# Sparse attention and a gated MLP on one core: the scores of three batches in three parts, and a new order on four engines

## The chip, the core and the metric

The kernel runs on one core of a Trainium2 chip. Five engines of that core work side by side, each through its own queue of instructions in order: TensorE (matmuls, PE in the profile), VectorE (DVE), ScalarE (ACT), GpSimd (POOL) and SyncE (SP, which only issues transfers here). GpSimd issues the loads, SyncE the stores and one kind of transfer inside the chip. The metric is the device time of one execution in microseconds; lower is better.

## The reference

```python
# q, k, v: (4 batches, 8 heads, 768 positions, 64), float32
k_sum = k.reshape(B, H, 24, 32, D).max(axis=3)
v_sum = v.reshape(B, H, 24, 32, D).mean(axis=3)
scores_l = scale * q @ k^T, kept where |i - j| < 16
scores_s = scale * q @ k_sum^T + log(32)
a = softmax(concat([scores_l masked, scores_s]))
attn = a @ concat([v, v_sum])
x = attn as (3072 tokens, 512)
h = x @ w_in                                  # 512 to 2048
g = h * clip(h + 3, 0, 6) / 6
out = g @ w_out                               # 2048 to 512, float32
```

Every position attends to its neighbours within 16 and to 24 block summaries; the result goes through one gated MLP over all 3,072 tokens.

## The kernel before

Queries are taken in 12 blocks of 64 per head. A block sees a window of 96 keys and the 24 maxima of the blocks of keys, so its scores are 120 rows: `kaug` holds 96 window keys and 24 maxima for each block, `qT` the queries with their positions shifted by 16, `at` the exponentials of the scores, `vaug` the values with a column of ones and the 24 block sums.

The work is cut into steps, and a key names each instruction (or short group) of a step: `s111.0` is instruction 0 of step s111. The steps are

- `c`: constants; `K`, `Q`, `V`, `H`, `I`, `O`: loads by GpSimd (k, q, v, the shifted part of v, w_in, w_out);
- `k0` to `k3`, `q0` to `q7`: transposes of k and q on TensorE and copies from PSUM (batch 0, and q of batch 1); `w10` to `w33`: transposes, copies and maxima of k (and of q for batches 2 and 3) on VectorE and ScalarE;
- `s`: scores on TensorE, exp on ScalarE, the mask on VectorE. Batch 0: `s0` pair of heads, half; in its first half the mask is added by two matmuls called cover (instruction 0), and the scores are instruction 1. Batches 1 to 3: `scores4`, keys `s` batch, pair of pairs, half. One call takes 6 blocks of 4 heads, 48 matmuls of 32 rows and 64 columns, into both `S` slots, then two exps of 768 elements a row and two masks;
- `h`: copies of the halo of v inside `vaug`; `u`: block sums of v and their spreading; `v`: values, reciprocal, scale, then transposes of the result (`xtr`) and copies into x. `v41` is the second half of batch 0. From x number 4 on (`LATE`), the transposes are done by VectorE (`blocks`, into y) and 16 transfers of SyncE per x (`move`, instructions 4 to 7 of `v201`, `v211`, `v301`, `v311`);
- `F` s `x` ft: x number s (0 to 7, 384 tokens each) times one 128-column slice of w_in, four matmuls of 384 columns, relu on ScalarE (instruction 1), gate on VectorE (instruction 2). For s = 0 and ft below 5 (`SPLIT`) the four matmuls are separate keys;
- `G` s ts `x` 0: 128 tokens times w_out in four parts of four matmuls, a copy (instruction 4) and a store (instruction 5).

PSUM holds three `h` slots, one `o` and two `S` slots of two banks. A slot is given to a step when its first instruction is issued and comes free after its last.

The text `ORDER` lists all keys, and the kernel issues its instructions in exactly that sequence, so each engine's queue is the part of the list that belongs to it. `:A` and `:D` choose ScalarE or VectorE where either can do a copy. Tokens that start with `~`, `-`, `_` or `=` are fillers (`keep`): matmuls of the constant tile idle into a free slot, whose result nobody reads. `~n`, `-n` and `_n` are n matmuls of 512, 128 and 64 columns; `=n` is one of n times 64 columns.

Of the kernel before, what the change touches and what calls it, by code (L numbers as in the profile page):

```python
# [37 lines left out]
F0x8.1 F0x8.2 F0x5.1 I0.0 F0x5.2 F0x11.0 F0x1.0 F0x11.1 F0x11.2 F0x1.1 F0x1.2 F0x1.3 F0x1.4 F0x1.5 v410.0 v410.1 F0x7.0 F0x7.1
F0x7.2 v410.2 F0x10.0 F0x10.1 I12.0 F0x13.0 F0x13.1 F0x15.0 F0x15.1 F0x13.2 F0x10.2 v411.3 v411.4:D v410.3 v410.4:A F0x15.2
F0x14.0 F0x14.1 F0x14.2 F0x9.0 F0x9.1 F0x9.2 F0x0.0 F0x0.1 F0x2.0 F0x2.1 K13.0 K10.0 c.12:A F0x0.2 K12.0 K11.0 w10.0 Q1w1.0  # L40
F1x14.0 F1x14.1 F1x14.2 F1x4.0 F1x4.1 F1x4.2 F1x2.0 F1x2.1 F1x2.2 w10.1:D F0x2.2 F0x2.3 F0x2.4 F0x12.0 F0x12.1 F0x12.2 F1x8.0
# [772 lines left out]
```

## Time and profile before

| what | value |
| --- | --- |
| median of 3 runs | 217.21 us (217.05 to 217.39) |
| profiled execution, span | 215.4 us |
| TensorE busy | 207.6 us, 96% |
| VectorE busy | 162.1 us, 75% |
| ScalarE busy | 136.0 us, 63% |
| GpSimd busy | 49.7 us, 23% |
| data moved by transfers | 22.68 MB |

The time of the profiled execution is known as its span only, from the first to the last instruction; the runs' times also hold what lies around it. In rows of the timeline the first number is the start in us from the span's start, the second the length, then the engine, the line, the operation and its tiles; in square brackets stands the idle time before it and what ended it. In grouped rows the two numbers behind the bar are the busy time in us and the mean duration in ns.

### The profile page before, as it was taken

Reading aid. Unit: us, or ns where it says so; the run is one execution under the profiler, and the core shown is the slowest. Engines: PE = TensorE matmul, PEld = TensorE weight load, DVE = VectorE, ACT = ScalarE, POOL = GpSimd, SP = SyncE. Lnnn points to the kernel's source line nnn. Section 1 sums busy time; section 2 is a strip of 40 time slices with the busy share of each in tenths; the row PEclk is TensorE's granted clock in tenths of the full one; section 3 lists DMA queues with packets and bytes.
Section 4 is the critical chain, followed back from the end, with each engine's and each line's share of the span. In section 5 each row is a group of like instructions: output and inputs, shape, how many; then the busy total and the mean of one; then the engine's idle time right before and its main releaser. Section 6 shows DMA issues by size and latency. Waiting matters only on the chain.

```text
span 215.4 us, 6065 instructions
## 1 busy us (share of the span) xinstructions
PE 207.6 (96%) x2521; PEld 119.9 (56%) x2548; DVE 162.1 (75%) x318; ACT 136.0 (63%) x264; POOL 49.7 (23%) x66
## 2 busy tenths in 40 slices
PE   7999999999999999999999999999999999999993
PEld 7556656655555565565555555555555555564442
DVE  6889889999899999898899889887865555640021
ACT  3879778887898988756578696566345355520110
POOL 7968347905753244000000000000000000000000
PEclk9999999999999999999999999999999999999999
DMA  5999999999999999930334234113314300013123
GB/s 75 161 155 188 204 187 171 191 201 163 204 160 194 181 121 151 107 146 11 37 37 143 27 37 110 49 22 38 70 21 80 76 0 17 34 49 122 52 85 134
DMA packets 91724, 22.68 MB, mean 105 GB/s; under 512 B 82224, under 2 KB 88752, under 8 KB 91696
## 3 DMA queue, kind: packets, MB, share of 16 engines
q0 software_dynamic: 62288, 14.41, 71.9%
q1 hardware_dynamic: 29264, 7.80, 15.3%
q8 instruction: 20, 0.33, 0.6%
q10 hardware_dynamic: 144, 0.07, 0.1%
q14 instruction: 8, 0.07, 0.1%
HBM read 28.82 MB, written 6.29 MB: 163 GB/s over the span
## 4 chain that ended last, share of the span: by engine, by line
PE 82%; SPq 5%; DMA 4%; issue 2%; DVE 2%; POOL 2%; ACT 1%; ACTq 0%; POOLq 0%
PE h L666 36%; PE o L683 29%; PE h L683 5%; SPq L648 4%; DMA first<-in_q_dram 3%; PE S L623 3%; PE S L512 2%; DMA out_dram<-ot 1%; ACT vaug L241 1%; POOL first L305 1%; PE S L636 1%; PE S L666 1%; PE h L581 1%; PE S L489 1%; PE S L553 1%
## 5 line engine op out<-in xcount | busy, mean ns | idle before, releaser
L666 PE MATMUL h<-x,win 128*128 128x384 bf16 x500 | 91.1, 326 | 0.1
L670 ACT ACTIVATE r<-h 128x384 f32<-128x384 f32 x125 | 58.7, 492 | 38.8 <-PE h L666 36.8
L671 DVE SCALAR_TENSOR_TENSOR g<-r,h 128x384 bf16<-128x384 f32 x125 | 65.9, 546 | 22.6 <-ACT r L670 20.0
L683 PE MATMUL o<-wout,g 128*128 128x512 bf16 x309 | 78.0, 379 | 1.9 <-issue 0.8
L666 PEld LDWEIGHTS <-win 128*128 128x128 bf16 x512 | 48.7, 98 | 35.5
L683 PEld LDWEIGHTS <-g 128*128 128x128 bf16 x400 | 38.4, 98 | 37.6 <-issue 0.3
L520 ACT ACTIVATE at<-S 120x768 bf16<-120x768 f32 x24 | 18.6, 810 | 5.5 <-PE S L512 5.4
L241 ACT COPY ot<-o 128x512 f32<-128x512 f32 x17 | 10.0, 587 | 15.4 <-PE o L683 14.2
L521 DVE TENSOR_TENSOR at<-at,mask 96x768 bf16<-96x768 bf16 x24 | 12.6, 549 | 2.0 <-ACT at L520 1.6
L605 DVE TENSOR_TENSOR xn<-S,rc 128x768 bf16<-128x768 f32 x14 | 13.3, 950 | 0.3
L343 POOL DMA_DIRECT2D vaug<-in_v_dram x10 | 11.9, 1194 | 0.4 <-DMA first<-in_k_dram 0.2
L241 DVE COPY ot<-h 128x512 f32<-128x512 f32 x2 | 1.3, 686 | 13.7 <-PE h L683 13.7
L683 PE MATMUL h<-wout,g 128*128 128x256 bf16 (+1 forms) x64 | 11.4, 326 | 0.0
L467 DVE TENSOR_REDUCE red<-kaug 128x24 bf16<-128x768 bf16 x12 | 11.2, 943 | 0.1
L241 ACT COPY vaug<-vaug 32x640 bf16<-32x640 bf16 (+3 forms) x17 | 8.9, 574 | 0.6 <-DMA vaug<-in_v_dram 0.3
L241 ACT COPY vaug<-vs 24x1536 bf16<-24x1536 bf16 x6 | 8.8, 1468 | 0.6 <-DVE vs L241 0.5
L782 PE MATMUL o<-idle 128*128 128x64 bf16 (+2 forms) x70 | 7.5, 287 | 1.1 <-DVE idle L287 1.1
L455 DVE STREAM_TRANSPOSE kaug<-kraw 128x768 bf16<-128x768 bf16 x8 | 8.1, 1025 | 0.3 <-PE S L512 0.3
L623 PEld LDWEIGHTS <-at 120*64 120x64 bf16 x336 | 6.3, 111 | 3.0 <-issue 1.6
L333 POOL DMA_DIRECT2D kraw<-in_k_dram x8 | 5.9, 740 | 8.5 <-DVE kaug L455 7.4
L642 DVE STREAM_TRANSPOSE y<-xn 128x768 bf16<-128x768 bf16 x8 | 7.6, 965 | 0.2
L512 PEld LDWEIGHTS <-kaug 32*128 32x128 bf16 x576 | 5.3, 92 | 4.4 <-issue 3.6
(108 smaller groups left out, 184.2 us busy)
## 6 DMA issues: line engine op xcount, KB each, us to landing
out_dram<-ot SPq DMA_DIRECT2D x19, 256.0 KB, 2.3
vaug<-in_v_dram POOLq DMA_DIRECT2D x6, 384.0 KB, 12.9
wout<-in_moe_w_out_dram POOLq DMA_DIRECT2D x4, 512.0 KB, 9.9
win<-in_moe_w_in_dram POOLq DMA_DIRECT2D x3, 512.0 KB, 10.0
kraw<-in_k_dram POOLq DMA_DIRECT2D x8, 192.0 KB, 12.4
x<-y SPq DMA_DIRECT2D x64, 24.0 KB, 2.0
first<-in_k_dram POOLq DMA_DIRECT2D x6, 192.0 KB, 12.3
first<-in_q_dram POOLq DMA_DIRECT2D x6, 192.0 KB, 12.3
```

The costliest lines, as they stand in the source:

```text
L241: {"ACT": nc.scalar.copy, "DVE": nc.vector.tensor_copy, "POOL": nc.gpsimd.tensor_copy}[eng](o, i)
L343: op("POOL", "dma128", lambda: nc.gpsimd.dma_start(out=o[BLK:WIN, a:z, 0:D], in_=rows[:, a:z]), w=[("v", b % 2, c) for c in range(lo, hi)] ...
L467: op("DVE", "max", lambda: nc.vector.tensor_reduce(red.slot[:], w[:, :, BLK:WIN].rearrange("p t (n c) -> p t n c", n=2), axis=AX.X, op=ALU ...
L512: nc.tensor.matmul(X[g // 2].slot[:, g % 2, i * QB:(i + 1) * QB], kaug[2 * u + m][rows, t], qT[rows, 2 * u + m, t * QB:(t + 1) * QB], star ...
L520: op("ACT", "exp", lambda a=a, e=e: nc.scalar.activation(a, X[e].slot[0:KEYS, :, 0:HALF], AF.Exp, scale=scl), r=[X[e]], w=[("at", p, half)])
L521: op("DVE", "masking", lambda m=m: nc.vector.tensor_tensor(m, m, mask[:, low(half):low(half) + HQ].unsqueeze(1).to_broadcast([WIN, 2, HQ, ...
L605: nc.vector.tensor_tensor(o, src[..., 0:D], r.unsqueeze(len(r.shape)).to_broadcast(list(o.shape)), op=ALU.mult)
L623: nc.tensor.matmul(X.slot[64 * c:64 * c + 64, i, m:m + D + 1], a[:, t * QB:(t + 1) * QB], vaug[b % 2][0:KEYS, h, t, 0:D + 1], start=True, ...
L666: nc.tensor.matmul(bank(h)[:, 0:HALF], w_in_sb[:, kt, cols], xt[s].slot[:, kt], start=(kt == 0), stop=(kt == NP - 1))
L670: op("ACT", "relu", lambda: nc.scalar.activation(r.slot[:], bank(h)[:, 0:HALF], AF.Relu, bias=0.5, scale=1.0 / 6.0), r=[h], w=[r])
L671: op("DVE", "gate", lambda: nc.vector.scalar_tensor_tensor(gt[s].slot[:, ft], r.slot[:], 1.0, bank(h)[:, 0:HALF], op0=ALU.min, op1=ALU.mul ...
L683: nc.tensor.matmul(o.slot[:, a:z], gt[s].slot[:, ft, ts * 128:(ts + 1) * 128], w_out_sb[:, ft, a:z], start=(ft == 0), stop=(ft == NFT - 1))
```

## The change

`scores4` takes a part in place of a pair of pairs and a half. Parts 0 and 1 are heads of one pair of pairs, query blocks 4 to 11: 64 matmuls, 512 columns in each of the four banks, two exps of 1024 elements a row, and two masks of 1024. Part 2 is query blocks 0 to 3 of all eight heads: again 64 matmuls, two exps of 1024, and four masks of 512. So there are three calls per batch, keys `s10`, `s11`, `s12` and so on, where there were four. The four tiles `at` become one tile, of which `at[p]` are slices, so that one exp can write two of them. Only part 2 reads the first 16 columns of `qT`, so only it waits for the copy `around` (now its own key, `qa`). Step `values` reads `at` by the new parts.

The list `ORDER` is replaced as a whole. GpSimd's sequence stays as it was through the loads of batch 1 (`V12`, `V10`); behind them it changes: before K20 K21 K22 K30 K23 V22 H2 Q22 V20 ..., after Q20 Q23 K22 K21 Q22 K23 K20 V22 H2 V20 .... TensorE, VectorE, ScalarE and SyncE get a new sequence throughout, some copies change between ScalarE and VectorE, and the fillers are others.

```diff
+    THIRD = NQ // 3
-    at = [sb([128, 2, S], BF16, f"at{p}") for p in range(NP)]
+    ats = sb([128, NP, 2, S], BF16, "at")
+    at = [ats[:, p] for p in range(NP)]
...
-    def scores4(b, u, half):
+    def scores4(b, part):
         X = [Buf("S"), Buf("S")]
+        us, ts = ((0, 1), (0, THIRD)) if part == 2 else ((part,), (THIRD, NQ))
+        n = (ts[1] - ts[0]) * QB
+        cols = slice(ts[0] * QB, ts[1] * QB)
         def mms():
-            for i in range(HQ):
-                t = low(half) + i
-                for m in range(2):
-                    for g in range(4):
+            for u in us:
+                for i, t in enumerate(range(*ts)):
+                    lo = us.index(u) * n + i * QB
+                    for m in range(2):
+                        for g in range(4):
                             ...
+        for e in range(2):
+            ps_ = [2 * u + e for u in us]
+            o = ats[0:KEYS, ps_[0]:ps_[-1] + 1:2, :, cols]
+            op("ACT", "exp1024", ... activation(o, X[e].slot[0:KEYS].rearrange("p j (u c) -> p u j c", c=n), AF.Exp, scale=scl) ...)
+            for p in ps_:
+                op("DVE", f"masking{n}", ...)
...
-        for half in range(2):
-            for u in range(2):
-                scores4(b, u, half)
+        for part in range(3):
+            scores4(b, part)
```

The list up to the first gates of x number 0, before and after:

```diff
-c.0 K00.0 c.7 c.17 c.6 c.8:A K01.0 c.10:D c.5 c.1 _40 -15 k0.0 k0.2:A c.18 ~1 =2 k1.0 K02.0 ~12 =3 k2.0 k3.0 c.15:D c.2 c.3
-s000.0 k0.3:A c.13:D c.4 c.11:A k1.1 Q00.0 q0.0 k1.4 k0.1 c.20 k1.2:A Q01.0 ~2 =5 q1.0 k0.4 k1.3:D c.9:A c.14:A c.19 k2.3:A
-q0.1:A s000.1 q0.2:A =1 s010.0 s010.1 k2.2:A k3.2:D k3.3:D k3.1 V00.0 h000.0:D h001.0:D k2.1 k2.4 s000.2 ~2 =5 v00.0 V01.0 u0.0
-h010.0:D s020.0 c.16 s010.2 q1.2:A u0.3:D u0.1:D u0.4:D v01.0 v01.1 v01.2 v00.1 q1.1:A V02.0 h020.0:A h021.0:A h011.0:A v00.2
-s020.1 v01.3 v00.3 V03.0 u1.0 u1.3:A h030.0:D s030.0 k3.4 ~2 s030.1 u1.4:D v01.4 h031.0:D Q0w0.0 Q0w1.0 v01.5:D Q0w2.0 =1 q3.0
-q3.1:D q2.0 u1.1:A u1.2:D s020.2 v02.0 v02.1 v02.2 s021.0 v02.3 s030.2 v03.0 v03.1 q2.1:A v03.2 s011.0 v03.3 v00.4 v00.5:D v02.4
-s021.1 s011.1 s021.2 v03.4 v03.5:D s011.2 v02.5:A s031.0 s031.1 s001.0 s031.2 I2.0 F0x3.0 F0x3.1 F0x3.2 F0x3.3 F0x3.4 F0x3.5
-I4.0 F0x6.0 F0x6.1 F0x6.2 F0x4.0 F0x4.1 F0x4.2 F0x4.3 v411.0 v411.1 F0x5.0 F0x4.4 F0x4.5 v411.2 s001.1 I8.0 u0.2:A s001.2 F0x8.0
...
+c.0 K00.0 K01.0 c.1 c.19 c.7 c.17 c.13:D c.14:A _40 -13 k0.0 K02.0 c.2 k0.2:A k0.3:A c.15:A c.5 c.3 Q00.0 k0.1 k0.4 c.4 c.20
+c.18 =7 s000.0 s010.0 k1.0 ~9 =6 k3.0 c.16 Q01.0 k1.2:A c.6 k1.3:A c.11:D k1.1 k1.4 V00.0 V01.0 V02.0 k2.0 k2.1 V03.0 ~3 =3
+q0.0 Q0w0.0 Q0w1.0 c.8:A k3.2:A k3.3:A Q0w2.0 q0.1:A ~1 =7 s000.1 q0.2:A s010.1 c.9:D q1.0 s000.2 s010.2 q1.1:A k2.2:A k3.1
+k2.4 h000.0:D s030.0 v00.0 s020.0 u0.0 q1.2:D c.10:D k3.4 k2.3:D u0.1:A u0.3:A I2.0 I4.0 h010.0:D s030.1 s020.1 v00.1 v01.0
+v01.1 s020.2 h020.0:D v00.2 v00.3 I8.0 v01.2 v01.3 v02.0 I0.0 s030.2 h021.0:A =1 v00.4 =4 u1.0 u1.1:A v00.5:D u0.2:D h030.0:D
+v01.4 v02.1 v02.2 v02.3 v03.0 u1.3:A v03.1 v03.2 v03.3 h011.0:A v01.5:A =6 q2.0 q2.1:D v02.4 q3.0 I12.0 K13.0 v03.4 h001.0:A
+K10.0 v02.5:D K12.0 q3.1:A s011.0 K11.0 F0x3.0 F0x2.0 Q1w1.0 F0x2.1 s021.0 u0.4:D s011.1 Q1w4.0 u1.2:D v03.5:D u1.4:D h031.0:D
+s011.2 s021.1 F0x2.2 F0x2.3 s031.0 s031.1 s021.2 F0x3.1 F0x3.2 F0x3.3 s001.0 s031.2 F0x5.0 F0x3.4 F0x3.5 Q1w2.0 F0x2.4 v411.0
+F0x2.5 Q1w0.0 v411.1 F0x7.0 F0x6.0 s001.1 s001.2 v410.0 F0x5.1 F0x5.2 F0x6.1 F0x8.0 O0.0 v411.2 v411.3 Q1w5.0 F0x7.1 v411.4:A
+F0x6.2 F0x9.0 F0x9.1 F0x7.2 v410.1 v410.2 F0x11.0 F0x4.0 F0x4.1 F0x4.2 F0x8.1 c.12:A F0x4.3 v410.3 F0x9.2 F0x10.0 F0x8.2
+F0x14.0 F0x11.1 Q1w3.0 v410.4:D F0x10.1 F0x11.2 F0x4.4 F0x14.1 F0x0.0 F0x10.2 F0x0.1 F0x0.2 O1.0 F0x12.0 O2.0 F0x12.1 F0x4.5
+F0x14.2 F1x10.0 F1x10.1 F1x0.0 O3.0 F1x0.1 F0x12.2 V12.0 F1x10.2 F0x0.3 F0x1.0 F0x1.1 F0x1.2 F1x13.0 F0x1.3 F1x0.2 V10.0 F1x3.0
+w10.0 F0x0.4 F1x13.1 F0x15.0 F0x1.4 F1x3.1 F1x13.2 F1x3.2 F0x15.1 F0x15.2 F0x0.5 F0x1.5 F1x7.0 F1x9.0 F1x8.0 F1x7.1 w10.1:A
```

And of the list after, the stretches around batch 1's second score group, the first turn of batch 2, the moves of x number 4 and its first F:

```diff
+F1x5.1 G02x0.1 s10.0 F1x5.2 F1x11.1 F1x12.1 s10.3 F1x11.2 F1x12.2 w13.0 w13.2 w12.2 w12.3:D F1x14.0 F1x2.0 F1x6.0 s10.1 F1x2.1
+w12.1:A G02x0.2 w13.1:A w13.3:A s10.4 G02x0.3 h120.0:D s10.2 G02x0.4:A s11.0 F1x6.1 s11.1 G00x0.0 G00x0.1 s11.3 Q20.0 h130.0:A
...
+G01x0.1 V22.0 u4.1:D u4.3:D u4.2:D u4.5:D v100.0 v100.1 u4.4:A v100.2 v101.0 v101.1 G01x0.2 G01x0.3 v101.2 v100.3 F1x14.1
+h131.0:A h111.0:D v101.3 G01x0.4:A G12x0.0 v100.4:A v101.4:D s12.0 F1x14.2 F1x6.2 s12.4 F2x10.0 F2x8.0 F2x8.1 w22.0 F2x15.0
...
+F3x10.2 v201.0 v201.1 v200.0 K32.0 Q31.0 F3x1.0 F3x2.1 F3x2.2 v201.2 F3x1.1 H3.1:A w21.5:A F3x1.2 v200.1 v200.2 w22.5:D F3x12.0
+F3x7.0 F3x7.1 F3x7.2 F3x12.1 F3x12.2 G11x0.5 G22x0.1 F3x6.0 s22.0 F3x6.1 v201.3 F3x14.0 F3x0.0 G22x0.2 F3x6.2 v200.3 v201.5
...
+F3x0.2 F3x8.2 w30.3 F3x14.2 F3x5.0 G20x0.3 w33.0 v210.2 F3x9.0 G20x0.4:A F3x13.0 F3x9.1 F3x13.1 v211.1 F3x9.2 v210.3 F3x5.1
+w33.2:A F3x13.2 G21x0.0 G21x0.1 G21x0.2 G21x0.3 w31.0 u6.5:A F3x5.2 F4x6.0 G21x0.4:A w31.3 w31.1 F4x8.0 F4x8.1 F4x14.0 G32x0.0
```

More of the change, by code (lines that the diff above doesn't have):

```diff
@@ L38 @@
[L38 to L41, printed above, removed]
@@ L86 @@
+G61x0.5 G71x256.5 G71x256.6
 """
@@ L472, in turn, with ats_of @@
         if b > 1:
[L473 removed]
+            op(EITHER, "around", lambda eng: copy(eng, qT[:, p, 0:PAD], qT[:, p, S:S + PAD]), r=[("q", p, 0)], w=[("qa", p)])
+    def ats_of(p, half):
+        return [("at", p, x) for x in ((1, 2) if half else (0,))]
     def scores(b, p, half):
```

115 lines of the change are left out of this document (52 added, 63 removed).

## The prediction

> **What bounds the kernel now.** I read the page's busy shares first, then the busy time of each engine in stretches, then TensorE's timeline, then the transfers.
>
> ```profile
> PE 207.6 (96%) x2521; PEld 119.9 (56%) x2548; DVE 162.1 (75%) x318; ACT 136.0 (63%) x264; POOL 49.7 (23%) x66
> DMA  5999999999999999930334234113314300013123
> ```
> ```profile
> 0.00:5.00 5.00, 3.87 (x57) 3.67 (x57) 3.09 (x13) 2.12 (x2) 3.64 (x13) 1.00 0.47 69
> 34.00:60.00 26.00, 25.55 (x404) 14.46 (x408) 24.30 (x48) 21.85 (x41) 16.10 (x18) 1.00 1.80 187
> 100.00:150.00 50.00, 49.31 (x659) 27.34 (x653) 43.35 (x79) 35.49 (x67) 0.00 (x0) 1.00 0.30 54
> ```
>
> The columns are stretch, length, busy PE, PEld, DVE, ACT, POOL, granted clock, DMA share, GB/s. From 34 us on TensorE is busy over 98% of the stretch, so it sets the end, and only two things move it: the matmuls it is given and the gaps it is made to wait. VectorE is at 93% from 34 to 60 and the transfers are full until about 90 us: the second and third limits. The front is where there is something to find: before 24.4 TensorE looks busy because it multiplies a constant (`keep`, tile idle).
>
> ```profile
> 1.13 3.92 PE L782 MATMUL o<-idle 128*128 128x64 bf16 x55 [1.13 <-DVE idle L287]
> 4.98 0.85 PE L391 MATMUL h<-ident,first 96*64 96x96 bf16 x16
> 6.41 0.54 PE L391 MATMUL h<-ident,first 96*64 96x96 bf16 x16
> 6.88 2.85 PE L782 MATMUL o<-idle 128*128 128x512 bf16 x13
> 9.66 0.53 PE L391 MATMUL h<-ident,first 96*64 96x96 bf16 x16
> 10.46 0.50 PE L481 MATMUL S<-bias,ident 96*128 96x384 bf16 x2
> 12.49 0.53 PE L420 MATMUL h<-ident,first 96*64 96x96 bf16 x16 [0.39 <-DMA first<-in_q_dram]
> 14.65 0.38 PE L581 MATMUL h<-vaug,at 96*64 96x65 bf16 x12
> 14.96 0.85 PE L535 MATMUL o<-vaug,ind 96*32 96x128 bf16 x24
> 24.39 2.12 PE L666 MATMUL h<-x,win 128*128 128x384 bf16 x12
> 27.24 0.28 PE L623 MATMUL S<-vaug,at 120*64 120x65 bf16 x6 [0.32 <-issue]
> 33.98 1.46 PE L666 MATMUL h<-x,win 128*128 128x384 bf16 x8
> ```
>
> Starts are taken from these rows: ends are modelled, so a group's cost is the distance to the next start. Thirteen wide fillers take 9.66 - 6.88 = 2.78, or 0.214 us per 512 columns. q1, the transposes of the second half of q, waits for its load at 12.49.
>
> **Matmuls and fillers.** The score matmuls stay 576: 12 groups of 48 become 9 of 64. The orders list 19 fillers of 512 columns before and 13 after (-1.28 us), 17 units of 64 columns before and 34 after (+0.45), and 13 in place of 15 of 128 columns in the cold start (55 fillers, 4,480 columns, took 3.85: -0.22). That is -1.05 us, and it is only a gain if what the fillers covered ends earlier too.
>
> **The front, walked to where it can be compared.** New order on TensorE: two start fillers less put k0 at 4.8 (its load lands at 1.36 + 3.4). k0 (0.85), a 448-column filler and two covers of batch 0's mask bias (s000.0, s010.0, 0.35 each, under the 0.50 of their row at 10.46) bring k1 to 6.6; 0.47 for it (6.41 to 6.88) and 9.75 wide fillers at 0.214 bring k3 and k2 to 9.2 and 9.6, q0 after 3.4 fillers to 10.7. Then s000.1 and s010.1, which stood behind q1, wait for ScalarE's two copies of q: it is free of k3's copies at 11.3, takes 0.86 (row below), and s010.1 is done at 12.5. There q1 starts, as before. So TensorE enters q1 with two score groups and the cover of s010 more behind it.
>
> ```profile
> 11.46 0.86 ACT L241 COPY qT<-S 128x384 bf16<-128x384 bf16 x2 [0.47 <-PE S L420]
> 13.43 1.00 DVE L241 COPY vaug<-vaug 32x768 bf16<-32x768 bf16 x3 [0.44 <-DMA vaug<-in_v_dram]
> 14.96 0.74 POOL L373 DMA_DIRECT2D win<-in_moe_w_in_dram  x1 [0.52 <-DMA vaug<-in_v_dram]
> 17.48 1.48 POOL L373 DMA_DIRECT2D win<-in_moe_w_in_dram  x2 [0.50 <-DMA vaug<-in_v_dram]
> win<-in_moe_w_in_dram POOLq DMA_DIRECT2D x1, 512.0 KB, 8.7
> ```
>
> From q1 the loads of v set the pace, and GpSimd's order, so their landing, is the same: the first at 13.4, the next at 15.0, the last at 17.5 (what GpSimd and VectorE waited for). v00.0 follows the first halo copy at 13.8 (14.65 before), u0 the second load at 15.0 (14.96 before), u1 the last at 17.8. Behind u1 stand two values groups with their sums, four small transposes, q2 and q3, each about 0.3 (14.65 to 14.96 for the first kind), in step with VectorE's scales (about 0.55, as the mask row below) and copies (0.33 by the row at 13.43): I get F0x3.0 at 21.7, after a wait for q2's copy, and the last score group of batch 0 done at 24.1, by when F0x3 and F0x2 (8 quarter steps, 1.30 us) are done too. Before, the scores are done at 24.39 and those steps would be done at 25.69: -1.5 us. F0x5 needs the second load of w_in: 14.96 + 8.7 = 23.7, in time by half a us.
>
> Part of it is given back. v411.0 needs the mask multiplications s021.2 and s031.2, and VectorE, by 0.55 each behind three spreads and two copies of the front, ends them near 25.4: 0.5 us of wait, where before has 0.32 at 27.24. After it F0x9, F0x10 and one transpose wait 0.15 to 0.25 each for VectorE. Before, the groups from 24.39 to 33.98 sum to 8.71 of 9.59 us, 0.88 lost; by this walk after loses 1.24 up to F0x10 at 31.5. Sum at 34 us: -1.5 + 0.36 = **-1.1**, little over what the missing fillers are worth.
>
> **The stream: scores in three parts.**
>
> ```profile
> 106.16 1.03 PE L683 MATMUL o<-wout,g 128*128 128x512 bf16 x4
> 107.02 1.46 PE L666 MATMUL h<-x,win 128*128 128x384 bf16 x8
> 108.32 1.03 PE L683 MATMUL o<-wout,g 128*128 128x512 bf16 x4
> 109.28 0.55 PE L512 MATMUL S<-qT,kaug 32*128 32x64 bf16 x48
> 112.46 0.85 PE L553 MATMUL S<-vaug,ind 96*32 96x128 bf16 x48
> 113.24 1.04 PE L623 MATMUL S<-vaug,at 120*64 120x65 bf16 x48
> 128.37 0.55 PE L512 MATMUL S<-qT,kaug 32*128 32x64 bf16 x48
> 128.85 2.12 PE L666 MATMUL h<-x,win 128*128 128x384 bf16 x12
> ```
> ```profile
> L670 ACT ACTIVATE r<-h 128x384 f32<-128x384 f32 x125 | 58.7, 492 | 38.8 <-PE h L666 36.8
> L520 ACT ACTIVATE at<-S 120x768 bf16<-120x768 f32 x24 | 18.6, 810 | 5.5 <-PE S L512 5.4
> L521 DVE TENSOR_TENSOR at<-at,mask 96x768 bf16<-96x768 bf16 x24 | 12.6, 549 | 2.0 <-ACT at L520 1.6
> ```
>
> Four G matmuls take 0.86 (106.16 to 107.02), so those at 108.32 end at 109.18; the scores start at 109.28. Entering a score group costs 0.10 us, its 48 matmuls 0.48 (128.37 to 128.85). Three entries less: **-0.3**; the matmuls cost 12 x 0.48 = 9 x 0.64, nothing. ScalarE: relu of 384 against exp of 768 gives 0.83 ns an element over 0.17 us, so 1.02 us for 1024, and 18 x 1.02 replaces 24 x 0.81: -1.1 us of ScalarE, hidden at 63% busy. Bounds for one: 0.81 (no longer) to 1.62 (two of 768). The masks keep their 18,432 columns and their 24 instructions, 12 of 1024 and 12 of 512; from the 0.549 row I take +0, with +-1.6 us of VectorE as bounds (0.549 for a 512 too, or half of it), hidden by VectorE's idle sevenths from 100 us on and partly exposed at 34 to 60.
>
> Places in the new stream follow from F0x10 at 31.5 by adding groups in their order: F 0.16 a matmul, G 0.216, values 0.44 a group of 24 and sums 0.78 (the rows at 112.46 and 113.24 hold 48 each), 0.10 for each entry. Two kinds of wait come in. s11.0, the second score group of batch 1, needs three copies that stand on ScalarE behind both longer exps of s10: s10 ends at 48.8, two exps (2.0), a relu (0.45) and copies of some 1.8 in all make 53.0, and TensorE is there at 52.5. If ScalarE's copies overlap as its relus do, the wait is nothing. I take **+0.35** for it and its like.
>
> ```profile
> 100.03 10.68 SPq L648 DMA_DIRECT2D x<-y  x16
> x<-y SPq DMA_DIRECT2D x64, 24.0 KB, 2.0
> ```
>
> The other kind: batches 2 and 3 are scored earlier (batch 3's sums, u6, at 101.9 against 112.46), and F4, F5 and F6 follow their x at once. SyncE issues sixteen moves, the last 10.0 us after the first, and 2.0 later it has landed: 12.0 us behind y. F3x6 starts at 95.9, its gate ends at 97.6, VectorE's last transposition of y at 99.0; so x4 stands at 111.1, and F4x6.0 comes at 112.4. In the same way x5 (y at 119.0) stands at 131.0 for F5x15.0 at 132.2, x6 (136.4) at 148.4 for F6x7.0 at 149.5. Before starts its moves at 100.03 for an F4 that its order puts near 117, 5 us to spare. The three reserves of 1.1 to 1.3 us are thin but whole: 0.
>
> **The end.** A 256 KB store is issued about 0.5 us later against the last matmul than before, beside the two last small ones: **+0.1** (0 to 0.4).
>
> Sum: -1.1 - 0.3 + 0.35 + 0.1 = **-1.0 us**: span 215.4 to 214.4. The profiled execution's time is known as its span; the median of the runs is 217.21, 1.8 us more for what lies around it, which does not change. Predicted: **216.2**. Its own range, with the front wrong by 0.5 and the waits by 0.5: 215.3 to 217.1.
>
> **The rivals.**
>
> *GpSimd's later order stalls VectorE (slower).* Batch 2's k now comes after two loads of q, and its last quarter, K20, after seven loads behind V10.
>
> ```profile
> 41.23 2.13 POOL L333 DMA_DIRECT2D first<-in_k_dram  x3 [0.15 <-issue]
> first<-in_k_dram POOLq DMA_DIRECT2D x1, 192.0 KB, 14.9
> 51.46 0.71 POOL L333 DMA_DIRECT2D first<-in_k_dram  x1
> first<-in_k_dram POOLq DMA_DIRECT2D x1, 192.0 KB, 9.8
> 64.27 1.03 DVE L455 STREAM_TRANSPOSE kaug<-first 128x768 bf16<-128x768 bf16 x1
> ```
>
> The first load behind V10 lands at 56.1 (41.23 + 14.9) and K23, four loads on, at 61.3 (51.46 + 9.8): 1.3 us a load. Six more than the first put the new K20 at 63.9. VectorE reaches the first turn of batch 2, w22.0, near 64.7 (v101 ends at 60.8 on TensorE, then two recips and scales, two copies, two gates); before, its first such turn is at 64.27, 3 us after its data. VectorE takes its instructions in order, so behind a late load stand the gates of F2, and then TensorE's three h buffers: 0.6 us of cover, so from a landing at 65.3 each us costs one. At 1.9 us a load it lands at 67.5: +2.2 - 1.0, **218.4**. For it: the reserve shrinks from 3 us to 0.8. Against it: the queue was full all along, and 1.3 us a load held over five loads. The same would come of a thin reserve of x4 to x6 that doesn't hold. Chance 0.20.
>
> *The front is bound by its chain of loads and copies (nothing much gained).* The missing fillers become idle time, and F0 is as late as before; only the entries are saved and the waits added: -0.3, **216.9**. For it: v411 and the gates wait for VectorE in my own walk, and VectorE and the v loads hardly change. Against it: TensorE's queue behind q1 is shorter by two score groups and a cover, and q1 is not later. Chance 0.20.
>
> *No new waits at all.* If the order fits as closely as the old one does from 100 us on (0.7 us not busy in 50), the 0.35, the 0.1 and half of the 0.9 lost at the start of F0 go too, -0.9 more: **215.3**. Against it: s11.0's copies. Chance 0.12.
>
> *The clock falls.* Fewer fillers mean idle TensorE. The start shows the price: 4,480 columns in 3.85 us, 0.86 ns each against 0.42 later, though the granted clock there reads 1.00. If one wait sets it back for as long, +2.0 - 1.0: **218.2**. My longest new wait is 0.5 us. The Trainium skill (TensorE: Matmul & The Clock Gate, "Why this matters for your kernels") asks that no idle gap exceed about 3 us, or the clock halves; by that rule too nothing falls here, and no run here shows a gap that long. Chance 0.03.
>
> **How the numbers follow.** The forecast has 0.45. The range takes in its own bounds, the second and third rivals and the near half of the first: 215.1 to 217.9. About 0.2%, 0.43 us, is what a measurement of this kernel can tell from no change. Faster by more: 0.42 of the forecast's 0.45, the 0.12, and 0.06 of the second rival, 0.60. Same: 0.03 and 0.12, 0.15. Slower: 0.02 of the second rival, the first and the last, 0.25.
>
> **What would show it.** Right: q1 at 12.5, first F0 matmul near 21.7, the last batch-0 scores near 24, 0.5 us of wait at v411; nine score groups of 0.64; exps of 1.0 us; last matmul ended about 1.1 us earlier. Wrong: F0 not before 22.5 with TensorE idle; VectorE waiting for first from in_k near 64; TensorE waiting for x near 112, 132 or 150.

## The result, and the profile after

The change made the kernel slower: 222.71 us median (222.13 to 223.43, 4 runs) against 217.18 us for the kernel before on the same chip (217.05 to 217.39, 4 runs), a ratio of 1.0256 [1.0232, 1.0280]. Forecast were 216.2 us (215.1 to 217.9) and a gain: wrong in sign and outside the range. The profiled execution took 222.13 us with a span of 220.4 us, against a span of 215.4 us before. Executions of one kernel differ by the clock that TensorE was granted in the front; where a median would mix them, times are given with their mean clock.

The granted clock in tenths on the page before (40 slices of the span):

```profile
PEclk9999999999999999999999999999999999999999
```

From the page after, TensorE's busy slices and the granted clock in tenths (one slice is 5.5 us), then the groups that answer to the exps and masks of before:

```profile
PE   7987999999989999999998999999999999999993
PEclk9998599999999999999999999999999999999999
...
L530 ACT ACTIVATE at<-S 120x1024 bf16<-120x1024 f32 x18 | 17.7, 1023 | 2.4 <-PE S L521 1.2
...
L534 DVE TENSOR_TENSOR at<-at,mask 96x1024 bf16<-96x1024 bf16 (+1 forms) x24 | 12.7, 545 | 1.7 <-ACT at L530 1.3
```

The work is as forecast (exps of 1.02 us, masks of the same sum); what is new is the 5 in the clock's row. The same in stretches (columns as in the prediction; the clock is the third number from the end), first the kernel before, then the kernel after:

```profile
13.60:20.40 6.80, 6.67 (x156) 4.66 (x155) 5.88 (x20) 6.32 (x13) 5.17 (x8) 1.00 2.04 172
```
```profile
13.60:20.40 6.80, 5.14 (x145) 3.95 (x141) 6.04 (x17) 4.66 (x10) 5.10 (x7) 1.00 2.09 171
20.40:27.30 6.90, 6.66 (x90) 4.66 (x87) 5.02 (x14) 4.45 (x10) 2.84 (x5) 0.51 1.29 204
27.30:34.00 6.70, 6.70 (x107) 4.03 (x106) 5.89 (x13) 5.11 (x10) 3.44 (x5) 1.00 1.79 183
```

For 6.9 us TensorE ran at half its clock (three other executions have a mean clock of 0.975 to 0.977, which is 10 to 11 us at one half), right after 6.8 us in which it had been busy for only 5.14, where the kernel before has 6.67. TensorE's timeline of the changed kernel: first the front, then every wait of over 0.25 us behind it.

```profile
13.15 0.53 PE L422 MATMUL h<-ident,first 96*64 96x96 bf16 x16
...
14.94 0.38 PE L594 MATMUL h<-vaug,at 96*64 96x65 bf16 x12 [0.71 <-DVE vaug L243]
...
17.65 0.38 PE L594 MATMUL h<-vaug,at 96*64 96x65 bf16 x12 [0.34 <-DVE vaug L243]
...
19.62 0.85 PE L548 MATMUL h<-vaug,ind 96*32 96x128 bf16 x24 [0.56 <-ACT vaug L243]
...
22.28 0.54 PE L594 MATMUL h<-vf,at 24*64 24x65 bf16 x12
...
25.54 1.14 PE L679 MATMUL h<-x,win 128*128 128x384 bf16 x3
...
29.45 0.57 PE L636 MATMUL S<-vaug,at 120*64 120x65 bf16 x24
...
57.31 0.24 PE L521 MATMUL S<-qT,kaug 32*128 32x64 bf16 x8 [0.47 <-issue]
...
61.04 0.85 PE L566 MATMUL S<-vaug,ind 96*32 96x128 bf16 x48
...
64.66 0.97 PE L636 MATMUL S<-vaug,at 120*64 120x65 bf16 x48 [0.93 <-DVE vaug L243]
...
118.75 2.11 PE L679 MATMUL h<-x,win 128*128 128x384 bf16 x12 [0.71 <-DMA x<-y]
...
156.22 2.11 PE L679 MATMUL h<-x,win 128*128 128x384 bf16 x12 [0.29 <-issue]
```

v00, v01 and u1 wait for halo copies, twelve values matmuls then take 0.54 in place of 0.38, F0x3 begins at 25.54 where 21.7 was forecast, and the stream (all that stands behind the front) has four waits where before's view of waits, from 34 us on, has five of at most 0.2 us each:

```profile
PE o L683 <- issue: 0.8, 5, 0.2
```

To see where the 5 us arose I compare the start of the sums of each batch with the work that stands ahead of it in TensorE's order, counted with one set of costs for every kernel (0.65 us for four F matmuls, 0.864 for four of G, 0.48 or 0.64 for a score group, fillers as in the prediction). Start minus work is a lag, and it grows only by waiting, by slow matmuls, or where this set of costs misses something:

| kernel | lag at u4 | at u5 | at u6 | at TensorE's end | fillers |
| --- | --- | --- | --- | --- | --- |
| before | 7.88 | 8.34 | 9.00 | 9.88 | 6.46 |
| after | 11.68 | 13.12 | 13.62 | 15.64 | 5.51 |

The front grew the lag by 3.80 (2.85 net of the 0.95 of fillers it dropped), u4 to u5 by 0.98, from u6 on by 1.14; between u5 and u6 after is 0.16 better. With 0.2 more behind the last matmul that is the 5.0 us between the spans.

### The profile page after: what moved, and what is told of

The parts are those of the page before. It is cut to its first block, busy times and chain, and to the rows that moved or that the text cites. A ratio compares the mean times of both kernels' runs of the same rounds, so it can differ in the third digit from the quotient of the medians.

```text
span 220.4 us, 6085 instructions
## 1 busy us (share of the span) xinstructions
PE 211.4 (96%) x2541; PEld 121.2 (55%) x2541; DVE 159.9 (73%) x311; ACT 135.6 (62%) x265; POOL 49.6 (22%) x66
## 4 chain that ended last, share of the span: by engine, by line
PE 81%; DVE 8%; SPq 5%; issue 2%; ACT 1%; DMA 1%; DVEq 0%
PE h L679 35%; PE o L696 28%; SPq L661 5%; PE h L696 5%; PE S L636 3%; PE S L521 2%; PE o L794 2%; DVE red L404 2%; DVE vaug L243 1%; DVE vaug L284 1%; PE S L649 1%; DMA x<-y 1%; PE S L679 1%; DVE g L684 1%; DVE y L655 1%
## 5 line engine op out<-in xcount | busy, mean ns | idle before, releaser
L683 ACT ACTIVATE r<-h 128x384 f32<-128x384 f32 x125 | 59.9, 492 | 39.9 <-PE h L679 37.7
L696 PE MATMUL o<-wout,g 128*128 128x512 bf16 x336 | 80.4, 379 | 0.0
L243 ACT COPY ot<-o 128x512 f32<-128x512 f32 x15 | 8.8, 585 | 23.1 <-PE o L696 21.1
L530 ACT ACTIVATE at<-S 120x1024 bf16<-120x1024 f32 x18 | 17.7, 1023 | 2.4 <-PE S L521 1.2
L534 DVE TENSOR_TENSOR at<-at,mask 96x1024 bf16<-96x1024 bf16 (+1 forms) x24 | 12.7, 545 | 1.7 <-ACT at L530 1.3
L243 DVE COPY ot<-h 128x512 f32<-128x512 f32 (+1 forms) x3 | 1.8, 603 | 16.6 <-PE h L696 16.6
L243 ACT COPY vaug<-vs 24x1536 bf16<-24x1536 bf16 x7 | 10.3, 1468 | 0.7 <-DVE vs L243 0.6
L243 DVE COPY ot<-o 128x512 f32<-128x512 f32 x6 | 4.1, 688 | 5.6 <-PE o L696 5.5
L636 PE MATMUL S<-vaug,at 120*64 120x65 bf16 x336 | 7.0, 196 | 0.9 <-DVE vaug L243 0.9
L243 ACT COPY vaug<-vaug 32x640 bf16<-32x640 bf16 (+3 forms) x14 | 7.5, 566 | 0.3 <-PE S L566 0.2
## 6 DMA issues: line engine op xcount, KB each, us to landing
kraw<-in_k_dram POOLq DMA_DIRECT2D x8, 192.0 KB, 12.7
first<-in_q_dram POOLq DMA_DIRECT2D x6, 192.0 KB, 13.4
```

Source lines behind the costliest of these rows:

```text
L243: {"ACT": nc.scalar.copy, "DVE": nc.vector.tensor_copy, "POOL": nc.gpsimd.tensor_copy}[eng](o, i)
L530: op("ACT", "exp1024", lambda o=o, e=e: nc.scalar.activation(o, X[e].slot[0:KEYS].rearrange("p j (u c) -> p u j c", c=n), AF.Exp, scale=sc ...
L534: op("DVE", f"masking{n}", lambda m=m: nc.vector.tensor_tensor(m, m, mask[:, ts[0]:ts[1]].unsqueeze(1).to_broadcast([WIN, 2, ts[1] - ts[0] ...
L636: nc.tensor.matmul(X.slot[64 * c:64 * c + 64, i, m:m + D + 1], a[:, t * QB:(t + 1) * QB], vaug[b % 2][0:KEYS, h, t, 0:D + 1], start=True, ...
L683: op("ACT", "relu", lambda: nc.scalar.activation(r.slot[:], bank(h)[:, 0:HALF], AF.Relu, bias=0.5, scale=1.0 / 6.0), r=[h], w=[r])
L696: nc.tensor.matmul(o.slot[:, a:z], gt[s].slot[:, ft, ts * 128:(ts + 1) * 128], w_out_sb[:, ft, a:z], start=(ft == 0), stop=(ft == NFT - 1))
```

## Experiments

The kernel before ran beside each; its median moved between 216.8 and 217.5 us from group to group, so differences between kernels of different groups are known to a few tenths. The ratios are each to the kernel before beside it.

### Front and stream apart

Two crosses. `c1` takes the order of before up to the exp of s031 and then the changed order, with three parts. `c2` takes the changed order that far, ends F0x3 and F0x2, and goes on as before, with four parts (v411.0 and v411.1 move ahead of F0x4).

```diff
 ... s031.0 s031.1 s001.0 s031.2      (before's front)
-I2.0 F0x3.0 F0x3.1 ...               (before's stream)
+I2.0 I4.0 I8.0 I0.0 u0.2:D I12.0 ... (after's stream, less what is done)
```

> The front of the kernel before (up to the exp of s031), then the order of the changed kernel for all that is left, with scores in three parts. The offset of the changed kernel's TensorE work grows by 5.2 us behind batch 0 where before's grew by 2.8. Theory F+S (front and stream each lose their own share, and the two add up): 219.4 (218.8 to 220.0), clock 1.00. Rival F (the whole loss comes from the front and only shows later): 216.5 to 217.3. Rival S (the stream loses it all): 221.5 to 222.7.

> The changed kernel's front (up to the exp of s031, with F0x3 and F0x2 ended right behind it), then the order of the kernel before for all that is left, with scores in four parts. Theory F+S: offset +3.4 by the front less 0.9 of fillers, so 219.7 (219.0 to 220.4) with the clock at one half for about 6.9 us. Rival S: 216.5 to 217.5. Rival F: 221.5 to 222.7.

c1 took 219.99 us median (218.29 to 221.32), 1.0104 [1.0042, 1.0165]: +2.5, clock 0.997 or more. c2 took 221.08 (220.34 to 221.82), 1.0170 [1.0132, 1.0207]: +3.6, clock 0.977 to 0.983; its range was 219.0 to 220.4, so the front cost more than the theory gave it. Neither half has it all: 2.5 and 3.6 make 6.1, against 5.5 together. The four executions of c1 lie 3.0 us apart, which their recorded clocks do not explain.

### The front: the clock and the chain

`a1` puts fillers where TensorE stood idle in the changed front; nothing else moves.

```diff
 ... s030.0 +~3 +=6 v00.0 ... v00.1 +~1 +=5 v01.0 ... +~3 u1.0
 ... v01.4 +~1 v02.1 ... v02.3 +~1 +=4 v03.0
```

> The changed kernel with fillers put where TensorE stood idle between 13.6 and 20.4 us of its front, ahead of v00.0, v01.0, u1.0, v02.1 and v03.0; nothing else moved. Theory G (the front's many short waits, none over about 1 us, were enough for the granted clock to fall to one half for 6.85 us, and that costs 3.4 us): the clock stays at 1.00 and the time falls from 222.7 to 219.6 (219.2 to 220.3, as a few fillers lie on the path). Rival C (the low clock only goes along with a front that waits for halo copies and loads; those waits end at the same time whatever TensorE does): 222.4 to 223.2, also where the clock shows 1.00.

220.70 us (220.13 to 221.15), 1.0139 [1.0104, 1.0175], clock 0.997 to 1.00. The low clock is gone and with it 2.0 us of the 3.1 expected (2.3 by the distance to the kernel before beside each); the fillers put 0.5 on the path (v00 at 15.41 in place of 14.94), and F0x3 begins at 25.12, only 0.4 earlier. So the clock was not all of the front.

The same fillers in c2, so that the stream is that of the kernel before:

> The changed kernel's front with its waits filled, then the order of the kernel before with four parts. Without the fillers this took 3.6 us over the kernel before, at clock 0.983. Theory: the clock is 0.995 or more and what is left is the front's chain of loads, halo copies and sums: 219.0 (218.3 to 219.7). Rival 1 (the clock was all of it): 217.0 to 217.8. Rival 2 (the chain is all of it): 220.4 to 221.3.

219.10 us (218.80 to 219.66), 1.0101 [1.0080, 1.0121]. Clock 0.999 or more, 2.0 under c2 (1.7 by the distance to the kernel before beside each), and 1.9 over the kernel before, in which the 1.4 us of fillers it has more than before (7.86 against 6.46) are contained: clock and chain both, as the theory said. The stretch from 13.6 us in c2, and the same stretch in this kernel:

```profile
13.60:20.40 6.80, 5.01 (x139) 3.92 (x140) 5.97 (x17) 4.43 (x9) 5.17 (x8) 0.96 2.06 172
```
```profile
13.60:20.40 6.80, 6.58 (x151) 4.29 (x150) 5.86 (x17) 4.18 (x9) 5.24 (x8) 1.00 2.07 171
```

TensorE is busy for 5.01 of 6.80 us and falls; busy for 6.58 it does not.

The opposite on the kernel before: `b2` takes out all fillers behind k0.0, `b3` only those behind the exp of s000, that is behind 13.9 us.

```diff
-~1 =2 ~12 =3 ~2 =5 =1 ~2 =5 ~2 =1   (b2: all of these, in their places)
-~2 =5 ~2 =1                         (b3: the last four)
```

> The kernel before, with all its fillers after k0.0 (early waits of TensorE) taken out and no instruction moved. Theory G: with its waits left empty the clock falls to one half for one or two stretches of 3.4 us between 14 and 28 us, and the time is 218.9 to 220.6 (one stretch +1.7, two +3.4). Rival C: the fillers only pass the time; 216.8 to 217.4 at clock 1.00.

> The kernel before, with only its last fillers taken out (those after the exp of s000, that is behind 13.9 us: 0.67 us ahead of v00, 0.5 ahead of s020, 0.2 ahead of q2), all earlier ones kept. Theory G (short waits between 14 and 20 us are enough): the matmuls of 18 to 28 us take the longer times seen in the changed kernel (0.54 for 12 of 65 columns in place of 0.38), and 218.6 to 220.6. Rival E (only the fillers of the first 12 us matter, which b2 took out too): 216.3 to 217.3, all rows at 0.38.

b2 took 222.71 us (219.73 to 222.79), 1.0200 [1.0131, 1.0269]: 5.3 more, where 1.7 to 3.4 had been expected, although 4.6 us of work were taken out. The profiled execution shows why it is so much: TensorE was never at full rate before 31 us.

```profile
9.00:31.00 22.00, 21.56 (x346) 15.30 (x347) 15.27 (x44) 14.55 (x28) 13.39 (x18) 1.00 1.74 182
```
```profile
10.64 0.82 PE L480 MATMUL S<-bias,ident 96*128 96x384 bf16 x2
...
23.37 0.54 PE L580 MATMUL h<-vaug,at 96*64 96x65 bf16 x12
```

The cover takes 0.82 us in place of the 0.50 before, the values 0.54 in place of 0.38. The record of this execution calls the clock 1.00; two others of the same time have 0.946, which is 24 us at one half.

b3 came out at 1.0012 [0.9975, 1.0049] over the seven executions at a clock of 0.984 or more: no difference that can be told. But the clock, which was what it tests, went both ways: five of ten executions are at 0.999 or more (216.64 to 217.41 us), two at 0.984 (217.69 and 219.54), three at 0.977 (220.81 to 221.32). The kernel before beside all the experiments had 0.992 or more in all of its 62 executions. So neither theory is right as it stood: where the clock holds, the late fillers are not needed for the time, but without them it falls in some executions and not in others, and the three at 0.977 took 3.8 to 4.3 us more than the median of the five (217.02).

`a2` brings VectorE's constants forward, into 3.1 to 7.0 us where it idled. In the changed kernel k1's reduce stood behind them at 10.62, and the first halo copy behind two more reduces (VectorE's timeline of after):

```profile
10.62 0.88 DVE L404 TENSOR_REDUCE red<-h 128x24 bf16<-128x768 bf16 x1
...
13.37 0.88 DVE L404 TENSOR_REDUCE red<-h 128x24 bf16<-128x768 bf16 x1
...
14.54 0.35 DVE L243 COPY vaug<-vaug 32x768 bf16<-32x768 bf16 x1
```

```diff
 ... c.5 +c.6 +c.20 +c.18 +c.16 +c.11:D c.3 Q00.0 +c.4 +c.9:D k0.1 k0.4 -c.4 -c.20 -c.18 =7
```

> The changed kernel with VectorE's constants earlier in its queue (five ahead of c.3, mask and edges ahead of k0.1), into the time where it idled. Theory V (the reduce of k1 behind the constants makes the halo copies late, TensorE waits for them, and the clock falls from that): h000 at 13.4, v00.0 at 13.8, clock 0.995 or more, 219.2 (218.6 to 219.8). Rival V1 (v00 is earlier by 1.1 us but the wait of u1 for ScalarE's halo copy stays, and with it the low clock): 221.3 to 221.9. Rival V0 (another instruction ends the wait): 222.3 to 223.2.

221.79 us (221.08 to 223.57), 1.0231 [1.0177, 1.0285]; clock 0.983. This is rival V1, but with other waits in the middle. TensorE's timeline of a2:

```profile
13.91 0.38 PE L593 MATMUL h<-vaug,at 96*64 96x65 bf16 x12
...
16.23 0.53 PE L493 MATMUL S<-qT,kaug 64*128 64x64 bf16 x24 [0.73 <-DVE kaug L408]
...
17.40 0.38 PE L593 MATMUL h<-vaug,at 96*64 96x65 bf16 x12 [0.34 <-DVE vaug L242]
...
19.29 1.46 PE L547 MATMUL h<-vaug,ind 96*32 96x128 bf16 x24 [0.20 <-ACT vaug L242]
```

v00 begins 1.03 earlier, then the scores of s030 and s020 wait 0.73 for a spread of k that stands on VectorE behind a q copy, which waited for ScalarE, and a constant, and u1, at 19.29, is only 0.33 earlier than in after. One instruction moved up in a full queue moves another wait in; the clock falls all the same.

### The stream: the moves of y

c1, with the old front, waits at the first product of tiles 4, 5 and 6 (its timeline; the third wait is put down to a gate of VectorE there):

```profile
114.94 2.11 PE L677 MATMUL h<-x,win 128*128 128x384 bf16 x12 [0.67 <-DMA x<-y]
...
135.30 2.12 PE L677 MATMUL h<-x,win 128*128 128x384 bf16 x12 [0.46 <-DMA x<-y]
...
153.32 2.11 PE L677 MATMUL h<-x,win 128*128 128x384 bf16 x12 [0.57 <-DVE g L682]
```

`c3` puts one G group ahead of each, `c4` also puts G01x0.2 ahead of v100.

```diff
 (c3)  +G21x0.4:A +G32x0.0 F4x6.0 ... +G30x0.4:A +G31x0.0 F5x15.0 ... +G42x0.2 F6x7.0
 (c4)  ... u4.5:D +G01x0.2 v100.0 v100.1 u4.4:A v100.2 v101.0 v101.1 -G01x0.2
```

> The old front with the changed kernel's stream, and one 512-column group (0.86 us) moved ahead of the first product of each of tiles 4, 5 and 6 (F4x6, F5x15, F6x7), which waited 0.67, 0.46 and 0.57 us there. Theory M (the order leaves 12.0 us between the last blocks of y and the use of x, and the moves take 11.1 to 11.9 and land later than that): the three waits end and the time falls by 1.7, to 217.8 in a run like the profiled 219.5 and to 218.3 at the median (217.6 to 218.7). Rival R (the wait goes elsewhere, as y of the next tile is later by as much): 219.3 to 220.2.

> As the one with the three groups moved, and the third 512-column group of G01 ahead of v100 too, where TensorE waited 0.88 us for VectorE's spreads of the sums of batch 1. Theory: 0.86 us less than that kernel (217.0 to 217.8), the cover taken from behind v101 being worth 0.3 or less. Rival: the transposes of v100 then wait for the scaled values by as much, and the time is that kernel's within 0.3.

Both were missed: 223.09 us (222.01 to 223.66), 1.0270 [1.0225, 1.0316], and 222.45 (221.96 to 222.89), 1.0249 [1.0218, 1.0279]. The waits for x are gone, but G32 needs the one `o` slot. TensorE, ScalarE and SyncE in c3:

```profile
117.44 1.02 PE L694 MATMUL o<-wout,g 128*128 128x512 bf16 x4 [1.97 <-ACT ot L241]
...
116.81 0.58 ACT L241 COPY ot<-o 128x512 f32<-128x512 f32 x1 [1.88 <-DMA out_dram<-ot]
...
102.44 11.93 SPq L659 DMA_DIRECT2D x<-y  x16
114.42 3.81 SPq L705 DMA_DIRECT2D out_dram<-ot  x4
```

Read upwards: the stores of earlier results stood in SyncE's queue behind sixteen moves until 114.42, so the buffer `ot` came free late, the copy out of PSUM waited 1.88 us, and the G group behind it 1.97. The experiment traded a wait of 0.7 for one of 2.0, so it does not say what the waits for x cost, but it named the resource: SyncE's queue.

`c6` is c1 with half of the moves issued by GpSimd, idle by then; `c7` adds the G01 group ahead of v100.

```diff
-                    nc.sync.dma_start(
+                    (nc.sync if c < 2 else nc.gpsimd).dma_start(
                         out=xt[s].slot[BLK * a:BLK * a + BLK]...
```

> The old front with the changed kernel's stream, and of each tile's 16 moves of y to x half issued by GpSimd's queue in place of SyncE's. SyncE issues 16 in 11.1 to 11.9 us, 0.74 each, and x4, x5, x6 came 0.67, 0.46 and 0.57 us late. Theory M (SyncE's issuing sets when x is there): the moves take about 6 us, the waits ahead of F4x6, F5x15, F6x7 end, and so do the waits of ScalarE's copies for stores queued behind the moves; 1.7 us less than the same without it: 218.3 at the median (217.5 to 218.8). Rival P (GpSimd issues them slower or they land later): 220 or more, with longer waits at the same places.

> As the one with half the moves on GpSimd, and the third 512-column group of G01 ahead of v100, where TensorE waits 0.88 us for VectorE's spreads. Theory: 0.6 us less than that kernel (0.5 to 0.9), 217.7 (217.0 to 218.2): what then still parts it from the kernel before is under 0.5. Rival: x4 to x6 are ahead by enough that nothing is gained or lost later, but the transposes of v100 wait: within 0.3 of that kernel.

c6: 218.25 us (217.10 to 219.28), 1.0042 [1.0012, 1.0073], as expected: 1.7 under c1 by the medians, 1.3 by the ratios, whose intervals overlap. Its waits for x are gone, that of tile 6 too. SyncE's and GpSimd's moves for tile 4:

```profile
102.29 5.54 SPq L659 DMA_DIRECT2D x<-y  x8
...
102.49 4.88 POOL L659 DMA_DIRECT2D x<-y  x8 [18.10 <-DVE y L653]
```

The lag from u6 to the end, 3.12 in c1, is 0.70, less than before's 0.88. Of the 2.4 us that this gains, 0.8 goes again at v100, which waits 1.72 here and 0.88 in c1's execution, with the same list up to there (1.82 in c3's, so this wait differs between executions). c7: 218.15 (217.27 to 219.35), 1.0043 [1.0015, 1.0072], the same as c6, as its rival had it: v100 waits 0.85 in place of 1.72, but its transposes then wait 0.62 for the scaled values, and the lag at u5 is 9.45 in place of 9.46.

### The stream: the spreads behind the sums

VectorE in the changed kernel around u4, whose matmuls begin at 61.04 and take 0.8:

```profile
61.60 0.80 DVE L243 COPY vaug<-vaug 32x640 bf16<-32x640 bf16 x3 [1.36 <-PE S L566]
62.42 0.69 DVE L534 TENSOR_TENSOR at<-at,mask 96x1024 bf16<-96x1024 bf16 x1
63.03 0.28 DVE L243 CAST vs<-S 128x128 bf16<-128x128 f32 x1
63.34 1.85 DVE L243 COPY vaug<-vs 24x1536 bf16<-24x1536 bf16 x3
```

VectorE idles 1.36 us for the sums, because two halo copies that must wait for them come next; then it does these and a mask it could have done in the idle time, and only then the copy of the sums for which v100 waits. `c8` is c6 with the mask ahead and the copy first:

```diff
 ... s11.4 K22.0 +s11.2 u4.0 +u4.1:D +h100.0:A +h110.0:D +u4.2:D +u4.3:D +u4.4:A +u4.5:D K21.0
-h100.0:A h121.0:D h110.0:D s11.2 ... u4.1:D u4.3:D u4.2:D u4.5:D ... u4.4:A
 ... v101.2 +h121.0:A v100.3
```

> The old front, the changed kernel's stream, half the moves on GpSimd, and behind the sums of batch 1 VectorE's copy of them first: the mask of s11 goes ahead of the sums (VectorE stood idle 1.21 us there), the halo copy of h121 to ScalarE behind v101. In the kernel without this the copy of the sums began 1.84 us after TensorE had ended them, behind two halo copies and the mask, and v100 waited 1.72 us for the spreads. Theory: the spreads are there by 60.3, v100 waits 0.2 or less, and the time is 1.5 less: 216.8 (216.3 to 217.3), at or just under the kernel before. Rival (ScalarE's spread of 1.47 us or the halos end later): 217.6 to 218.3.

217.32 us (217.07 to 217.70, 12 runs) against 217.16, a ratio of 1.0006 [0.9991, 1.0022]: 0.9 under c6 where 1.5 was expected, and level with the kernel before. In c8 the copy begins at 58.56, right when TensorE is done, and v100 and v101 still wait 0.48 in all:

```profile
58.56 0.29 DVE L241 CAST vs<-S 128x128 bf16<-128x128 f32 x1 [0.98 <-PE S L564]
...
60.96 0.57 PE L634 MATMUL S<-vaug,at 120*64 120x65 bf16 x24 [0.32 <-DVE vaug L241]
61.70 0.38 PE L634 MATMUL S<-vaug,at 120*64 120x65 bf16 x12 [0.16 <-DVE vaug L241]
```

`d1` puts both cures (moves and sums) into the changed kernel and leaves its front alone:

> The changed kernel with its front untouched; only the two causes found in the stream are taken away: half the moves on GpSimd, and VectorE's copy of the sums of batch 1 ahead of the halo copies, with the mask of s11 ahead of the sums. Theory (front and stream add): the low clock stays (0.985 or less) and 2.3 us come back, 220.4 (219.8 to 221.0). Rival (the stream's waits were slack that the late front only uncovered): 221.8 to 223.

Median 220.75 us (217.88 to 221.05), 1.0136 [1.0081, 1.0190]: 2.0 under the changed kernel, in the range forecast. Three executions at clock 0.974 or 0.975 took 220.66 to 221.05; one, at 0.999, took 217.88. The same program on the same chip, so about 3.0 us is the price of the low clock here, and 0.7 is left to the front's chain and the rest. One such execution is thin evidence for the 3.0; c2 against its filled version gave 1.7 to 2.0, with the fillers' own time in it, and b3 gave 3.8 to 4.3.

### All four at once, and three parts in the old order

`a4` is the changed kernel with a2's constants, fewer fillers than a1 (`~1 =4` ahead of s030.1, `=6` ahead of v01.0, one more `=4` ahead of u1.0), half the moves on GpSimd, and G01x0.2 ahead of v100.

> The changed kernel with all of it: VectorE's constants earlier, fillers in the waits left between 14 and 20 us, half the moves on GpSimd, the third group of G01 ahead of v100. Theory (the four causes add up): clock 0.995 or more, 222.7 - 0.9 - 1.6 - 1.2 - 0.6 = 218.4 (217.5 to 219.3), the rest being the front's chain of loads, copies and halos. Rival (the causes hide one another, so that less comes back): 219.8 to 221.

218.58 us (217.89 to 220.52), 1.0057 [1.0026, 1.0087]. 218.4 had been expected, so the causes add in the main. That it came so close is partly luck: 0.6 of the sum was for G01x0.2, and in c7 this move gave nothing. The clock is 0.997 or more in eight of ten executions, and 0.989 and 0.984 in the two slowest.

`b1` was meant to try three parts alone in before's order. It can't be had cleanly: the third part reads all of `kaug`, so its scores must precede the first turn of batch 2, and I had to pull the transposes of v100 and v101 ahead of it.

```diff
 ... +v100.3 +v100.4:A +v101.3 +v101.4:A +s12.0 +s12.1 +s12.4 w21.0
 ... +s12.2 +s12.3 +s12.5 +s12.6 w20.0 ... +w22.5:A s22.0
```

> The order of the kernel before (front, fillers, stream) with the scores of batches 1 to 3 in three parts: the third part of batch 1 stands ahead of the first turn of batch 2, with the transposes of v100 and v101 moved ahead of it, the others in the place of a quarter. Theory O (three parts cost nothing by themselves; the loss is all in the new order): 217.0 (216.6 to 217.6), three entries of 0.10 us less. Rival L (exps of 1.02 us in place of 0.78 hold the S slots longer and the third parts wait for them): 218.2 to 219.5, with waits ahead of s12, s22 and s32.

223.55 us (222.50 to 224.81), 1.0302 [1.0255, 1.0350]. Neither theory had that. TensorE's longest wait, the clock behind it, and VectorE ahead of it:

```profile
73.01 2.60 PE L677 MATMUL h<-x,win 128*128 128x384 bf16 x8 [2.15 <-DVE g L682]
```
```profile
73.00:76.50 3.50, 3.49 (x11) 1.61 (x11) 2.66 (x5) 0.98 (x2) 0.00 (x0) 0.52 1.82 180
```
```profile
65.36 1.04 DVE L455 STREAM_TRANSPOSE kaug<-first 128x768 bf16<-128x768 bf16 x1 [1.93 <-PE S L519]
67.99 0.56 DVE L682 SCALAR_TENSOR_TENSOR g<-r,h 128x384 bf16<-128x384 f32 x1 [1.58 <-ACT r L681]
```

VectorE's first turn of batch 2 stood idle for 1.93 us until s12's scores had read the old keys, which comes of the place that I gave s12; then a gate waited 1.58 us for a relu that stood on ScalarE behind both exps of s12. So the places and the longer exps are not told apart here, and b1 is inconclusive on three parts. It shows once more, far from the front, what a wait does: 2.15 us of idle time, then 3.5 us at half the clock. That three parts need not cost anything rests on c8, which has them and is level with before; c8 also has half of its moves on GpSimd, and no run tries that in the order of the kernel before.

## Why the prediction was wrong, point by point

**Matmuls, fillers, exps, masks, entries.** Right as amounts of work. 18 exps of 1.023 us (1.02 forecast); masks 12.7 us in all (12.6 before); a group of 64 scores takes 0.64 and its entry 0.10, so the 0.3 was there.

**The front, -1.1: failed.** Against the walk F0x3 was 3.8 us late (25.54 for 21.7). It was 1.1 late at v00 and 1.8 at u1; the other 2.0 came behind u1, most of it at the low clock (5.9 us from u1 to F0x3, where a1, with the clock up, needs 4.7 with 0.5 of added fillers in it). q1 began at 13.15 for 12.5 (the two covers ahead of k1 took 1.14 us, not 0.70), but v00 waited for VectorE anyway. Two steps of the walk were wrong. First, "v00.0 follows the first halo copy at 13.8": the copy was timed by the landing of v at 13.4, but in VectorE's queue it stands behind a reduce and a spread that end at 14.5, because the constants ahead of k1's reduce push all of them; v00 began at 14.94. Second, "the last at 17.8" for u1: its sums read rows that the halo copies write, and the last of these stood on ScalarE behind two exps; u1 began at 19.62. The second rival named this chain; it is real, but cost more than its 0.7: it fed the next point. The 0.5 of wait forecast at v411 did not come (29.45, without a wait).

**The clock, chance 0.03: the mechanism that decided.** Its price of 2.0 was near the 2 to 3 us of the runs; its condition was wrong. I asked whether one wait would be long, and my longest was 0.5. The trace has 0.71, 0.34 and 0.56 between 14.2 and 19.6 us, 1.66 us of 6.8 idle in all, and the clock fell. The section of the Trainium skill that I leaned on (TensorE: Matmul & The Clock Gate, "Why this matters for your kernels") warns of gaps over some 3 us; here no gap came near that and the clock fell all the same, so to keep below it is not enough, and the measurement decides. Two other sections of the page fit: "A second HAM failure mode: psum-queue depth-cycling" says that frequent short idle times between groups make the gate swing, and "What's actually happening" that it looks at free-running windows of about 3.4 us. The runs fit both: in after the clock is at one half for 6.9 us, in b1 for 3.5; mean clocks of 0.992, 0.984 and 0.977, which come up often, are 3.5, 7.0 and 10 us at one half of a 219 us span (0.989 to 0.991, in a4 and b1, lie between); and one program falls in some executions and not in others (b3, d1). The sum had taken the fillers for time to be saved; b2 shows that those of before hold the clock.

**x4 to x6, "thin but whole: 0": failed by size.** The time from y to use was 13.1 us without the wait (13.4 forecast): y's last block ended at 104.9, TensorE was free for F4x6 at 118.0. But x took 13.8, not 12.0. The moves' issuing lasted 11.92 us (10.68 in the row used), and x came 1.8 us behind its end (1.3 in the forecast). The rival that named GpSimd's loads mentioned this in a sentence, without a price. It cost 0.7 in after at tile 4 and 0.3 at tile 6 (there the profile names no releaser, but in d1, with the moves split, the wait is gone), and 1.7 in c1; taking it away gave 1.3 to 1.7 (c6).

**s11.0, +0.35: right in size, by luck.** After has 0.47 us of wait there, but not the one forecast. The last of ScalarE's copies is this row of its timeline:

```profile
55.72 0.45 ACT L243 COPY kaug<-red 128x288 bf16<-128x288 bf16 x1
```

It ended at 56.17 and s11.0 began at 56.23, when the matmuls ahead of it ended. The wait stands inside the group, behind 56 of its 64 matmuls, and the profile names nothing that ended it; c1, with the same stream, has none there. Its cause stays open.

**v100: missed.** The sum held no term for the order of VectorE's queue behind u4; it cost 0.93 in after.

**The first rival's place** (VectorE waiting for K20 near 64) did not show: no such wait is in the trace. **The end, +0.1:** 0.19.

In sum, of the 5.5 us: about 2.0 are the stream's two causes (d1), 2 to 3 the clock (a1 and d1), the rest the front's chain with what little the three parts save.

## What to carry to other kernels

A filler's worth is not the gap it covers but the clock it holds: before taking one out, add up the idle time of TensorE in the few microseconds around it (1.66 of 6.8 us in after, 0.22 in the filled front), not the longest gap. When an order is rewritten, walk the in-order queues of the helper engines (here VectorE's constants, halo copies and masks) behind every step that TensorE waits for, with all that they read. And a queue that issues many small transfers is a resource with a length: sixteen moves held SyncE for 11 to 12 us and, behind them, the stores, their buffers and a PSUM slot; splitting them over an idle queue was worth 1.3 to 1.7 us.

## What was not expected of the hardware

The granted clock in the record is not always the one the matmuls ran at: in b2's profiled execution it reads 1.00 while the rows of 9 to 31 us take 0.82 and 0.54 in place of 0.50 and 0.38, and the time is that of executions with 0.946. The Trainium skill (TensorE: Matmul & The Clock Gate, "Seeing it yourself") warns that these records can't be fully trusted; the trace agrees. Durations of a known row are the surer sign.

GpSimd issued eight moves in 4.88 us while SyncE needed 5.3 to 6.6 for its eight, so for these small transfers the one queue issued no more slowly than the other. The moves landed later when split, though: a median of 3.7 us (SyncE) and 3.3 us (GpSimd) after their issue in c6, against 2.1 in c1.

What stays open: how much idle time TensorE may have before the clock falls. From 13.6 us on, 5.14 busy of 6.8 us fell in after, 6.36 held in a1 and 6.58 in d2. In between, b3's profiled execution held with 5.50 (half of its executions fell), and a4's fell, for part of the 6.9 us that follow, with 5.95. So the busy share alone does not decide it.
